# A written-out order table of 1518 operations, replaced by another order of the same operations

## The chip, the cores and the metric

The kernel runs on one core of one Trainium2 chip. The metric is device time in microseconds (us). A core has a matrix engine (TensorE, called PE in the profile, with its weight loads shown apart as PEld), a vector engine (DVE), an activation engine (ACT), a general engine (POOL) and a queue engine for transfers (SP). POOL, SP and ACT can each issue transfers; 16 DMA engines move the data. Each engine runs its own list of instructions in order and waits on semaphores for the others.

## The reference

```python
scores = scale * np.matmul(q, k.transpose(0, 1, 3, 2))      # 8 batches, 8 heads, 576 x 576, head size 64
mask = block_i >= block_j                                   # blocks of 64 positions, causal by block
attn = np.exp(np.where(mask, scores, -1000000000.0) - rowmax)
attn = attn / (np.sum(attn, axis=-1, keepdims=True) + 1e-09)
x = np.matmul(attn, v)                                      # heads side by side: 8 x 576 x 512
h = np.maximum(x.transpose(0, 2, 1) @ w_tok1, 0.0) @ w_tok2 # 576 -> 256 -> 576, over the positions
u = x + h.transpose(0, 2, 1)
h2 = np.maximum(u @ w_ch1, 0.0) @ w_ch2                     # 512 -> 1536 -> 512, over the channels
out = u + h2
```

Attention goes first, then an MLP over the positions (token mixing), then an MLP over the channels. Inputs and output are 32-bit floats; the products run in bf16.

## The kernel before, in words

The kernel goes through the eight batches. For each batch it loads q, k and v, transposes q and k on DVE (L442), forms the scores of each half of the heads in sets on PE (L566), takes their exponentials on ACT (L585 for the first batch, L772 for the others), copies and clears the ends of rows (L594 and L599, on DVE or POOL), multiplies with the values on PE (L616 for a head, L669 for the row ends of a pair of heads) and divides on DVE (L636, L642). Token mixing follows (L807 and L811 up, relu at L793 on ACT or L795 on DVE, then L902 and L933 down), then channel mixing. There, some batches use a plain product (L1030), the others a product with sums of the weights and of the data that needs fewer multiplications (L1103 and L1230 up, L1364 down, with the sums at L1346 and the folds into the output at L1410 on DVE). The output rows leave by the transfers of L1439 and L1455.

Every step is recorded as an operation with a number, the engines that may do it, the operations that it needs, and the PSUM banks that it takes. Nothing runs until the table `ORDER` is read: one word for an operation, with its number, one letter for the engine (T is PE, A is ACT, D is DVE, P is POOL, S is SP), and one letter for each PSUM bank that it takes (a to d the pool "mm", e to h the pool "late", which exists once the scores of the first batch have left s and t). The order of the words is the order in which instructions are emitted, so it is also the order within each engine's list. The reader of the table is this:

```python
for word in ORDER.split():
    digits = word.rstrip("abcdefghstADPST")
    o, letters = self.ops[int(digits)], word[len(digits):]
    o.engine = self.ENGINE[letters[0]]
    ...
    assert all(d.n in done for d in o.deps)
```

So the table alone decides three things: the place of an operation in its engine's list, the engine where there is a choice (a copy out of PSUM may go to ACT or DVE, L400 and L402; a row-end copy to DVE or POOL; an output transfer to SP or ACT), and the PSUM bank.

Operations that are named below: 13, 16 and 19 are the first loads of k and q on SP, with the casts 14, 17 and 20 behind them (L400, L402) and the transposes 15, 18, 21, 23, 25 (L442); 22, 24, 26, 28, 30, 32 and 34 to 43 are further loads on POOL of q, k (L418, L437) and v (L468). 155 to 158 are the loads of the token weights, 159 to 169 and 421 to 437 those of the channel weights and of v and q, k of later batches. 44 is a run of 11 warm-up matmuls (L371), and 45 to 81 are fillers, single matmuls on zeros (L378). 174 is the first score set. 222, 223, 226, 227 are halves of head products of the first batch, 230 the row ends of its pair, and 269 and 281 score sets of the next batch; 281 is the first operation that takes the four late banks. 470 and 445 are score sets of a later batch and 505 a relu. 1037 is the load of the last piece of v of batch 6, 1044 a memset on POOL, 1134 another load. 1568 and 1590 are output transfers, and 1590 is the last operation.

## Time and profile before

| | before |
|---|---|
| median of three runs | 286.15 us (285.68 to 286.21) |
| the profiled execution, its own time | 287.38 us |
| span from the first to the last instruction | 285.6 us |
| PE busy | 275.0 us (96%) |
| weight loads of PE busy | 204.6 us (72%) |
| DVE busy | 238.6 us (84%) |
| ACT busy | 179.2 us (63%) |
| POOL busy | 72.4 us (25%) |
| mean granted clock of PE | 1.000 |

Busy time is the time in which an engine had an instruction in work. The chain of waits is the chain of work that ended last, followed back from the last instruction: at each step to what released it. "issue" in that chain is time in which an engine waited for nothing that the profile shows. A group of instructions has its line, engine, operation, what it writes and reads, the number of them, busy time, mean length of one in ns, and the idle time of the engine ahead of them with its releaser.

### The profile page before, as it was taken

The numbers are of one execution on the slowest core, as the hardware profiler recorded it, in microseconds if no ns is written. First come the engines' busy times: TensorE is split into PE (matmuls) and PEld (weight loads), VectorE is DVE, ScalarE is ACT, GpSimd is POOL, SyncE is SP. The second block draws the span as 40 slices with busy tenths as digits, with TensorE's granted clock in tenths as the row PEclk, the third lists the DMA queues.
The fourth block names the chain that finished last, engine by engine and source line by source line (L and its number), as shares of the span: only waits on it lengthen the run. The fifth ranks groups of instructions, "written<-read, shape, count | busy, mean of one in ns | idle before, by whom it ended". The sixth has DMA issues, their size and how long they took to land.

```text
span 285.6 us, 9588 instructions
## 1 busy us (share of the span) xinstructions
PE 275.0 (96%) x4089; PEld 204.6 (72%) x4110; DVE 238.6 (84%) x515; ACT 179.2 (63%) x331; POOL 72.4 (25%) x126
## 2 busy tenths in 40 slices
PE   8798899999998999999999999999999999999995
PEld 3466557488776777987877657856789976568884
DVE  3587578999898798999998979959897897579984
ACT  3798688962999664897779876073542734652200
POOL 8885661411621171055052120000000000000000
PEclk9999999999999999999999999999999999999999
DMA  7999999964999392999799397011043602100157
GB/s 166 170 171 179 202 191 203 132 107 101 111 93 141 65 141 45 155 222 157 88 102 165 31 181 90 16 61 21 0 76 73 223 0 76 73 2 2 73 149 221
DMA packets 64891, 31.97 MB, mean 112 GB/s; under 512 B 53200, under 2 KB 55888, under 8 KB 64848
## 3 DMA queue, kind: packets, MB, share of 16 engines
q0 software_dynamic: 44896, 17.49, 53.3%
q1 hardware_dynamic: 19520, 13.21, 19.0%
q8 instruction: 32, 0.52, 0.7%
q10 hardware_dynamic: 432, 0.66, 0.7%
q14 instruction: 11, 0.09, 0.1%
HBM read 35.85 MB, written 9.44 MB: 159 GB/s over the span
## 4 chain that ended last, share of the span: by engine, by line
PE 91%; ACT 3%; DMA 2%; issue 2%; DVE 1%; SPq 0%
PE late L1364 23%; PE mm L1103 8%; PE mm L1230 7%; PE mm L566 7%; PE mm L1364 7%; PE late L1230 6%; PE late L1103 6%; PE mm L616 5%; PE mm L807 3%; PE late L616 2%; ACT e_sb L585 2%; PE late L566 2%; PE late L902 2%; PE mm L902 2%; PE late L1030 2%; PE mm L1030 2%
## 5 line engine op out<-in xcount | busy, mean ns | idle before, releaser
L772 ACT ACTIVATE e_sb<-mm 128x512 bf16<-128x512 f32 x82 | 46.6, 607 | 14.0 <-PE late L566 10.2
L772 ACT ACTIVATE e_sb<-late 128x512 bf16<-128x512 f32 x86 | 48.5, 610 | 9.2 <-PE late L566 8.4
L442 DVE STREAM_TRANSPOSE qk_sb<-qk_sb 128x288 int32<-128x288 int32 (+1 forms) x65 | 41.4, 692 | 3.6 <-ACT qk_sb L400 1.6
L468 POOL DMA_DIRECT2D vals<-in_v_dram x45 | 36.9, 830 | 5.7 <-PE mm L616 2.4
L1364 PEld LDWEIGHTS <-gT 128*128 128x128 bf16 x336 | 32.0, 98 | 5.6 <-issue 0.4
L1364 PEld LDWEIGHTS <-sums 128*128 128x128 bf16 x324 | 31.3, 98 | 5.3 <-issue 0.4
L566 PEld LDWEIGHTS <-qk_sb 32*64 32x64 bf16 x1280 | 19.6, 104 | 13.9 <-issue 10.2
L566 PE MATMUL mm<-qk_sb 32*64 32x512 bf16 (+7 forms) x560 | 27.5, 289 | 0.4
L616 PEld LDWEIGHTS <-e_sb 128*128 128x128 bf16 x640 | 23.1, 97 | 6.5 <-issue 3.2
L566 PE MATMUL late<-qk_sb 32*64 32x512 bf16 (+7 forms) x560 | 26.8, 295 | 0.9 <-issue 0.6
L1364 PE MATMUL late<-wd_sb,gT 128*128 128x256 bf16 x168 | 20.7, 273 | 0.0
L1364 PE MATMUL late<-wd_sb,sums 128*128 128x256 bf16 x168 | 20.6, 273 | 0.0
L1103 PEld LDWEIGHTS <-ws_sb 128*128 128x128 bf16 x192 | 18.2, 98 | 3.1 <-issue 0.9
L642 DVE TENSOR_TENSOR x_sb<-mm,rinv 128x256 bf16<-128x256 f32 x45 | 18.7, 421 | 1.3
L616 PE MATMUL mm<-vals,e_sb 128*128 128x65 bf16 x450 | 19.5, 193 | 0.0
L1410 DVE TENSOR_TENSOR o_sb<-late,u_sb 128x512 f32<-128x512 f32 x22 | 14.9, 682 | 3.6 <-PE late L1364 3.6
L1230 PEld LDWEIGHTS <-ws_sb 128*128 128x128 bf16 x120 | 11.7, 98 | 8.6 <-issue 0.2
L1103 PEld LDWEIGHTS <-wc_sb 128*128 128x128 bf16 x144 | 15.3, 114 | 1.4 <-issue 0.4
L1364 PE MATMUL late<-wc_sb,gT 128*128 128x256 bf16 x132 | 16.2, 273 | 0.1
L594 POOL COPY vals<-e_sb 128x256 bf16<-128x256 bf16 (+1 forms) x11 | 4.3, 390 | 41.2 <-ACT e_sb L772 40.5
L400 ACT COPY mm<-late 128x512 f32<-128x512 f32 (+1 forms) x16 | 9.1, 571 | 8.1 <-PE late L1230 5.6
L793 ACT ACTIVATE gT<-mm 128x512 bf16<-128x512 f32 x21 | 12.6, 617 | 1.9 <-PE mm L1103 0.9
(198 smaller groups left out, 628.3 us busy)
## 6 DMA issues: line engine op xcount, KB each, us to landing
out_dram<-o_sb SPq DMA_DIRECT2D x19, 256.0 KB, 2.6
qk_sb<-in_k_dram POOLq DMA_DIRECT2D x14, 288.0 KB, 5.6
qk_sb<-in_q_dram POOLq DMA_DIRECT2D x14, 288.0 KB, 6.0
vals<-in_v_dram POOLq DMA_DIRECT2D x28, 128.0 KB, 4.4
out_dram<-o_sb SPq DMA_DIRECT2D x7, 512.0 KB, 3.5
wc_sb<-in_moe_w_ch_dram POOLq DMA_DIRECT2D x8, 192.0 KB, 7.8
wc_sb<-in_moe_w_ch_dram POOLq DMA_DIRECT2D x3, 512.0 KB, 10.8
vals<-in_v_dram POOLq DMA_DIRECT2D x15, 64.0 KB, 5.2
```

The costliest lines, as they stand in the source:

```text
L442: nc.vector.transpose(dst[:, 0:S, :] .rearrange("p s e -> p (s e)") .bitcast(I32) .rearrange("p (a k) -> p k a", k=NB)[:, k0:k1], raw2.bit ...
L468: nc.gpsimd.dma_start(out=t[128 - p : 128, J, hs, 0:64], in_=src)
L566: nc.tensor.matmul(out=home(n)[64 * half : 64 * half + 64, c : c + w], lhsT=bar[r, 0] if j is None else kT[i][r, 64 * j : 64 * j + 64, par ...
L616: nc.tensor.matmul(out=u[:, I, 0:65], lhsT=e[:, h, c : c + 128], rhs=vt[:, J, head, 0:65], start=(J == 0), stop=(J == I),)
L642: nc.vector.tensor_tensor(out=xt[:, 0:4, 64 * head : 64 * head + 64], in0=u[:, :, 0:64], in1=ri[:, 0:4].to_broadcast([128, 4, 64]), op=MULT,)
L772: nc.scalar.activation(dst, bank_of(x), EXP, scale=scale)
L793: nc.scalar.activation(dst, src, RELU)
L902: nc.tensor.matmul(out=bank_of(bank), lhsT=w2_sb[:, t, 128 * si : 128 * si + 128], rhs=at[:, t, :], start=(t == 0), stop=(t == NDT - 1),)
L1103: nc.tensor.matmul(out=bank_of(bank)[:, 256 * o_ : 256 * o_ + 256], lhsT=x(o_, m), rhs=y[:, :, m, :], start=opens, stop=m == 1, skip_group ...
L1230: nc.tensor.matmul(out=bank_of(bank)[:, 128 * c : 128 * (c + step)], lhsT=x(m), rhs=y[:, c : c + step, m, :], start=opens, stop=m == 1, sk ...
L1364: nc.tensor.matmul(out=bank_of(bank)[:, 256 * i : 256 * i + 256], lhsT=x[:, kk, 128 * i : 128 * i + 128], rhs=y[:, kk], start=first and i ...
L1410: nc.vector.tensor_tensor(out=dst, in0=src, in1=other, op=ADD)
```

## The change

The table is replaced by another one; no function changes. The new table has the same 1518 operations and so the same matmuls, loads and stores. What differs is their order, the choice of the engine for some of them, and the banks. It is three lines shorter, so that lines behind it have numbers lower by three. The diff, cut to the start of the table (some 30 us of work), the places named above, and its end:

```diff
@@ -98,84 +98,81 @@
 ORDER = """
-    13S 5P 9D 2D 3P 16S 44Ta 12P 19S 10P 4P 30P 22P 14D 24P 15D 17A 32P 1D 26P 18D 20A 28P 0A 45Tb 21D 252P 46Tb
-    47Tb 48Tb 49Ta 50Ta 37P 51Ta 52Ta 23D 53Ta 54Ta 25D 55Ta 56Ta 35P 57Ta 7D 174Tst 175T 34P 195A 58Ta 59Ta 60Ta
-    61Ta 196A 62Ta 38P 197D 63Ta 31D 64Ta 65Ta 66Ta 176A 199Tt 36P 177A 178D 67Ta 179D 68Ta 33D 69Ta 255P 70Ta 200A
-    180Ts 27D 198P 71Ta 72Ta 40P 73Ta 181A 29D 182Tt 157P 74Ta 75Ta 76Ta 183A 77Ta 201Ts 43P 78Ta 79Ta 80Ta 253D
-    202A 42P 214Tt 254D 188Tb 189T 41P 215A 184Tc 11D 233Ts 6D 190D 191D 258P 192Td 211Ta 234A 220Tt 216P 256D 39P
-    185T 257D 221A 81Tb 218Ts 155P 212D 213D 207Tb 235D 208T 186D 219A 158P 187D 237Tt 193D 209D 156P 203Ta 210D
-    204T 238A 194D 239Ts 261P 205D 206D 164P 8D 240A 236D 269Tcbda 424P 271A 163P 281Tefgh 270A 166P 259D 273A 217D
-    226Tb 283A 227T 284A 222Tc 223T 228D 241Ta 242T 282A 229D 165P 249Tf 224D 245Tg 285A 225D 162P 246T 230Tb 243D
-    244D 339Tc 159P 250D 231D 232D 337Ta 251D 247D 161P 340A 260D 272A 276Tbfeh 338D 348Tc 262D 160P 278A 349T 263D
...
-    362A 443D 359D 502Te 444P 483A 435P 393D 485A 604P 484A 504Td 503A 437P 170D 486A 470Tcbag 595P 505A 171D 601P
-    473A 445Tfehd 471A 172D 514Ta 448A 508Tc 472A 173D 515A 512Th 506Tb 446A 509D 510Ta 474A 513D 397Tcf 447A 475P
...
-    744A 981D 1022D 966Ta 984A 963Tc 1023D 745T 985A 967D 888D 1119P 986A 964D 965D 983A 1037P 995Td 968D 873A 998Tc
...
-    1056D 1075P 1057D 1015Tc 1134P 1068D 1146A 1127D 1013Ta 1145A 1069D 1102Th 1129D 1147A 1076D 1144A 1014D 1093Td
...
-    1556T 1588A 1567D 1562T 1569S 1557D 1586T 1563D 1568S 1587D 1590S
+    3P 10P 2D 9D 44Ta 45Tb 52Tc 56Td 1D 58Ta 46Tb 13S 14A 16S 15D 17D 18D 54Tc 4P 51Td 19S 12P 62Ta 5P 57Tb 50Tc 22P 23D
+    55Td 20A 21D 59Ta 64Tb 24P 30P 47Tc 25D 48Td 28P 66Ta 174Tst 175T 76Tb 60Tc 176A 177A 70Td 29D 49Ta 43P 74Tb 68Tc
+    71Td 195A 196A 180Ts 197D 75Ta 34P 53Tb 81Tc 26P 181A 198D 32P 182Tt 183A 80Td 37P 65Ta 31D 38P 199Ts 200A 27D 73Tb
+    33D 61Tc 201Tt 178D 35P 179D 202A 36P 188Td 184Ta 189T 190D 214Ts 192Tb 6D 191D 215A 252P 254D 233Tt 234A 185T 186D
+    187D 41P 203Tc 204T 253D 156P 205D 220Ts 221A 40P 211Td 206D 212D 218Tt 158P 219A 67Ta 207Ta 208T 209D 155P 237Ts
+    238A 63Tc 239Tt 255P 240A 78Tc 39P 79Tc 216D 42P 217D 222Tc 223T 213D 69Td 11D 256D 210D 257D 226Ta 193D 194D 157P
+    227T 228D 230Td 229D 281Tefgh 284A 283A 235D 236D 285A 337Tb 224D 225D 339Ta 282A 241Tg 231D 232D 242T 338D 340D
+    269Tcdfb 272A 243D 244D 341Th 261P 262D 263D 342D 245Ta 246T 247D 248D 348Te 349T 351Tg 271A 273A 350A 270A 352T
+    268P 258P 259D 276Tfdhb 164P 353A 280A 278A 249Ta 260D 160P 345Te 279A 346T 250D 251D 343Tc 277A 8D 301Tgabd 305A
...
+    503A 173D 504Tb 505A 470Tcgha 472A 77Te 471A 445Tfdeb 514Tg 512Tc 513D 447A 449A 506Td 508Tb 473A 474A 510Th 515A
...
+    640D 629Ta 630D 631D 572D 632Tb 72Td 573T 574A 635Tg 788Tdfha 791A 689S 633D 634D 790A 673Tc 636D 637D 674D 675D
...
+    993D 751T 994D 1043D 1119P 1036P 1083A 1005D 1006D 742D 752D 1085A 1084A 1045Tcgda 1124D 1046A 1044P 1047A 1049A
+    753T 1134P 1077Tehfc 1081A 1015Tg 1080A 1121D 754D 1078A 755T 1048A 1123D 1016D 1120D 1037P 1058Ta 1079A 1059D 1060D
...
+    1583D 1588A 1584T 1585D 1589A 1563D 1566T 1567D 1569S 1556T 1557D 1568A 1586T 1587D 1590A
 """
```

In numbers: 12 copies out of PSUM, net, go from ACT to DVE, 8 of the clips from DVE to ACT against 2 back, 5 row-end copies or memsets from DVE to POOL against 7 back. Output transfers on ACT's queue are 2 instead of 1 at L1439 and 4 instead of 2 at L1455; the last of all, 1590 (128 KB), is one of them. PE's instructions are the same 4110 pairs of a weight load and a matmul; the number of times that two neighbours on PE use different tile forms (such as 32x64 and 128x128) goes from 120 to 124. POOL issues the early loads in the order 22, 24, 30, 28, 43, 34 (before 30, 22, 24, 32, 26, 28) and so on, with 155, 156 and 158 earlier.

## The prediction

> **What bounds the kernel now.** I read the engine totals and the forty slices first, then the chain of waits, then windows of the stages where the chain leaves PE, and last single lines by form.

> ```profile
> span 285.6 us, 9588 instructions
> PE 275.0 (96%) x4089; PEld 204.6 (72%) x4110; DVE 238.6 (84%) x515; ACT 179.2 (63%) x331; POOL 72.4 (25%) x126
> PE   8798899999998999999999999999999999999995
> PEclk9999999999999999999999999999999999999999
> DMA  7999999964999392999799397011043602100157
> q8 instruction: 32, 0.52, 0.7%
> PE 91%; ACT 3%; DMA 2%; issue 2%; DVE 1%; SPq 0%
> ```

> PE carries 91% of the chain at a full granted clock in every slice. The change keeps PE's 4110 loads of weights and 4110 matmuls, with the same shapes. So only what PE waits for can move: its first operation on real data, gaps on the way, and what follows its last matmul. The chain shows these places (columns: start, length, what):

> ```profile
> 7.34 1.27 DVE qk_sb L442 x3
> 16.61 4.99 ACT e_sb L585 x5
> 21.64 0.66 PE late L566 x15
> 22.29 0.60 issue
> 28.27 1.09 issue
> 51.44 1.08 ACT e_sb L772 x2
> 53.50 0.50 ACT aT L793
> 57.26 1.31 PE late L1364 x12
> 59.15 1.42 PE mm L1364 x12
> 92.01 0.98 issue
> 282.08 0.42 DVE o_sb L1410
> ```

> Three steps are called "issue": PE waits for nothing that the profile shows, in the middle of an operation. Two rows of PE's timeline show where it resumes, and the windows from one stall to the next count its instructions (columns: window, length; then busy time and count of PE, PEld, DVE, ACT, POOL; clock, DMA share, GB/s).

> ```profile
> 22.89 0.38 PE L566 MATMUL late<-qk_sb 32*64 32x512 bf16 x1 [0.60 <-issue]
> 29.36 0.38 PE L855 MATMUL mm<-w_sb,aT 128*128 128x512 bf16 x1 [1.09 <-issue]
> 22.60:28.90 6.30, 5.32 (x127) 4.17 (x128) 4.97 (x17) 4.86 (x10) 3.19 (x6) 1.00 1.09 190
> 28.90:92.60 63.70, 61.93 (x1144) 44.39 (x1151) 55.10 (x128) 51.43 (x102) 24.67 (x40) 1.00 1.13 142
> 220.00:260.00 40.00, 40.00 (x287) 28.64 (x285) 31.56 (x50) 21.86 (x38) 0.00 (x0) 1.00 0.18 67
> 280.00:290.00 10.00, 2.05 (x19) 1.58 (x17) 1.71 (x5) 0.00 (x0) 0.00 (x0) 0.89 0.39 136
> ```

> Between the first two stalls lie 127 + 128 = 255 instructions, between the second and third 1144 + 1151 = 2295, within 9 of 9 x 256. The page's instruction queue moved 32 packets, and PE and PEld together ran 4089 + 4110 = 8199, or 256 for each packet. So I read the stalls as PE arriving at the end of a block of 256 instructions before the next block is there. All three lie where the DMA share of the window is at least 1.09; elsewhere the blocks come in time. From the first stall's end to the second's PE needed 29.36 - 22.89 = 6.47 us for one block.

> **The change part by part.** The sum goes from the profiled execution, 287.38 us with a span of 285.6; the median of the runs, 286.15, is 1.23 below it, and I carry the difference to that median.

> *(a) First score.* The first scores wait for three DVE transposes behind q's cast, 1.27 us in the chain. The new order puts the 160-column one before that cast, so two remain.

> ```profile
> L442 DVE STREAM_TRANSPOSE qk_sb<-qk_sb 128x160 int32<-128x160 int32 x1 | 0.5, 456 | 0.0
> 6.63 0.67 ACT L400 CAST qk_sb<-gT 128x576 bf16<-128x576 f32 x1 [1.47 <-DMA gT<-in_q_dram]
> ```

> That is -0.46 if q's load lands at the same time, and up to +0.5 if POOL's other order of loads (a q piece goes ahead of the pieces of k) slows it; the row shows ACT waiting 1.47 us for it. I take -0.3, nearer the transposes, which are certain.

> *(b) Work ready while ACT does the exps of the first batch.* The exps (4.99 us of chain) set when PE goes on at 21.64. By then the old order has done one more score set; the new one has done four head products and their ends instead, and leaves that set for later.

> ```profile
> 42.97 0.60 PE mm L616 x20
> 24.22 0.32 PE L669 MATMUL late<-vals,e_sb 128*64 128x65 bf16 x8
> ```

> The head products are such a group of 20, 0.60; the ends add about 0.3; a score set costs 0.5 (this one is narrow) to the 0.66 of the row at 21.64. So PE has 0.9 behind it instead of 0.5: -0.4, and as fewer fillers stand between, I take -0.5; bounds -0.9 (the set fits into a later gap) and 0 (the exps end later).

> *(c) The stalls at 22.29 and 28.27.* Blocks stay 256 long, so moving operations changes how much PE time a block holds. A stall is the time from asking for a block to having it, less PE's time until it gets there. I take the asking to be a block and a quarter (320 instructions) ahead, an assumption; then the old stalls answer to latencies of

> ```profile
> 16.27:22.60 6.33, 5.66 (x171) 3.36 (x164) 4.75 (x18) 6.27 (x9) 5.01 (x9) 1.00 1.43 159
> 20.96:28.90 7.94, 6.32 (x179) 4.53 (x160) 5.80 (x19) 6.50 (x13) 4.09 (x8) 1.00 1.12 180
> 85.29:92.60 7.31, 6.43 (x173) 4.59 (x159) 6.44 (x20) 6.75 (x14) 1.61 (x3) 1.00 1.42 145
> ```

> some 6.6, 8.4 and 7.7 us, each window counted on to the resuming matmul (22.89, 29.36, 92.99; the windows' counts take in a few instructions that overlap their start). Adding PE's times per operation along the new order, the 320 instructions ahead of the same two boundaries hold 6.73 and 5.65 us, where the old ones hold 5.04 and 5.59. At the first the new time exceeds the old latency, so no stall; at the second the stall is between 6.6 - 5.65 = 0.95 and 8.4 - 5.65 = 2.75, and I take 1.9, the middle, as which loads stand ahead differs. 1.9 against 0.60 + 1.09: +0.2, bounds -1.69 (no stall at all) and +1.06.

> [...]

> *(d) Other waits from 24 to 31 us.* With work pulled ahead, token-mixing operations meet their DVE copies sooner. In the old window between the stalls PE idles 6.30 - 5.32 = 0.98, of which the stalls' ends are 0.29 and 0.63. Bounds 0 and 0.7, one copy by DVE of 695 ns (row under (k)) that comes late; I take +0.2, as the old order shows nearly none.

> *(e) The wait through ACT at 53.5.* The chain passes over ACT from 51.44 to 54.00, because a relu stands between exps there. In the new order that relu has gone ahead and a filler stands between the two score sets. Bounds 0 and -0.50 (the row); I take -0.3.

> *(f) The stall at 92.01.* The 320 instructions ahead of that boundary hold 6.11 us in the new order, 6.42 in the old, so at the old latency it would be 1.6. But four loads of 288 KB stand queued ahead of it in the old order, from

> ```profile
> 81.24 0.56 POOL L418 DMA_DIRECT2D qk_sb<-in_k_dram  x1 [3.73 <-DVE gT L1157]
> 85.62 0.53 POOL L418 DMA_DIRECT2D qk_sb<-in_q_dram  x1
> ```

> and fewer in the new. Between the bounds of 0 and 2.3 (6.11 against the longest latency) I take 0.4, near the shortest, 6.6: -0.6.

> *(g) Four more changes of PE's tile form* (124 for 120). One costs 1.42 - 1.31 by the two L1364 rows, about 0.1; two fall where PE is full: +0.2.
> *(h) Fillers.* Their number stays, but two now stand at about 48 and 73 us, where PE is full, instead of in the wait for the exps:

> ```profile
> L378 PE MATMUL mm<-wd_sb 128*128 128x256 bf16 x37 | 5.2, 274 | 0.0
> ```

> 5.2 / 37 with overlap leaves some 0.1 each in a row of them: +0.2 (0 if PE would have waited there, as in (e)).
> *(i) A late piece of v.* POOL issues one piece of batch 6's values behind a memset that PE's progress releases, with 6.3 us of PE work until its first use, where 14.6 were. The first of these rows has the median time to landing of such a piece, the second that of a slow transfer on the same queue, and the last two belong to (j):

> ```profile
> vals<-in_v_dram POOLq DMA_DIRECT2D x15, 64.0 KB, 5.2
> wc_sb<-in_moe_w_ch_dram POOLq DMA_DIRECT2D x8, 192.0 KB, 7.8
> out_dram<-o_sb ACTq DMA_DIRECT2D x1, 128.0 KB, 2.5
> out_dram<-o_sb SPq DMA_DIRECT2D x1, 128.0 KB, 2.0
> ```

> By 5.2 it is in time, by 7.8 late by 1.5. +0.2, bounds 0 and 1.5.
> *(j) The last output.* It is issued from ACT's queue instead of SP's: 2.5 against 2.0 us to landing by the last two rows, but ACT is idle from 280 on. +0.1, bounds -0.1 and +0.5. [...]
> *(k) Copies and clips.* A net 12 plain copies from PSUM go from ACT to DVE, some clips and tails the other way:

> ```profile
> L402 DVE COPY mm<-late 128x512 f32<-128x512 f32 x5 | 3.5, 695 | 1.7 <-PE late L1230 1.0 <-PE late L1364 0.7
> L400 ACT COPY mm<-late 128x512 f32<-128x512 f32 x15 | 8.8, 585 | 7.8 <-PE late L1230 5.6 <-PE late L1364 2.2
> ```

> Over the kernel DVE gets about 6 us more (12 by 0.695, less what leaves), nearly all in 220 to 260: 31.56 + 5.8 = 37.4 of 40. PE covers this, being busy for all 40 us there; uncovered, it costs what case 4 says. 0.

> Sum: -0.3 - 0.5 + 0.2 + 0.2 - 0.3 - 0.6 + 0.2 + 0.2 + 0.2 + 0.1 = -0.6; 286.15 - 0.6 = 285.5.

> **The rivals.** *Case 2, no block stalls left.* The new table may also have moved loads away from the asking, so both remaining stalls vanish: -2.67 for the three stalls, and -0.2 for all other terms together: 283.3. For it: most blocks pass without a stall although the DMA engines are full. Against it: 5.65 us before the second boundary is short of every latency in the three windows.
> *Case 3, the blocks come later.* At the upper bounds of (c) and (f), 2.75 and 2.3, these are +1.06 and +1.32, with -0.2 for the rest: 288.3. [...] It decides from a latency of 8 us at the second boundary.
> *Case 4, DVE becomes the bound in 220 to 260.* It has 8.44 us idle there, 2.6 with the added copies. Its waits are for PE's products, which come in order, so part of that idle must stay: with all of it 37.4 + 8.4 - 40 = 5.8 us come on top, with half 1.6, with two thirds 3.0, which I take: 285.5 + 3.0 = 288.5. It decides where the idle cannot fall under 2.6. Against it: PE has no gap in the old window, so the copies have slack.
> *Case 5, nothing on balance.* What leaves one stall arrives in another: 286.15.

> **How the numbers follow.** About 0.2%, 0.57 us, is what a measurement of this kernel can tell from no change. Forecast .45 (own range 284.6 to 286.4, (c) and (f) off by 0.45 each; it splits .28 faster, .13 same, .04 slower); case 2 .18, faster; case 3 .16 and case 4 .12, slower; case 5 .09, same. Faster .46, same .22, slower .32. The range goes from case 2, with (d) and (i) at 0, 282.9, to case 3, 288.3; what lies outside is the far half of cases 3 and 4 and a little of 2.

> **What would show it.** In the new profile: the first scores at about 8.3 (7.34 + 1.27 - 0.3); PE's wait behind the exps ending near 21.3; no "issue" step near 22, one of about 1.9 us near 28, and one under 1 us near 92; no step over ACT near 53; DVE at 37 of 40 busy in 220 to 260 with PE still at 40. The prediction is wrong if the stalls sit at other boundaries or are longer, if PE shows gaps behind DVE late in the kernel, or if PE waits for a value load near batch 6's heads.

## The result, and the profile after

The changed kernel takes 298.31 us (median of 4, 294.95 to 299.17) against 285.91 us for the old one on the same chip: 1.042 times as long, 95% interval 1.033 to 1.050. The forecast was 285.5 us, in a range of 282.9 to 288.3. It is wrong in sign and far outside the range. Executions of one and the same kernel differ in the mean clock that PE was granted and, with it, in time (0.969 to 0.988 in the four of the new kernel), so the clock is given beside a time where that matters.

The profiled execution of the new kernel took 299.17 us. First its page:

```profile
span 297.4 us, 9596 instructions
PE 283.2 (95%) x4088; PEld 208.7 (70%) x4110; DVE 246.2 (83%) x524; ACT 178.9 (60%) x324; POOL 72.9 (25%) x124
PE   8799999999999899999999899999999999999974
PEclk9955999999999999999999999999999999999998
```

PE still does the same matmuls, but it is busy 8.2 us longer, and two of the forty slices of the clock stand at 5 where the old kernel had 9 everywhere. (The chain of this profile can be followed back to 54.7 us only, so its shares are not compared.) The windows of the two places where the clock is low (columns as before: window, length, busy time and count of PE, PEld, DVE, ACT, POOL, then clock, DMA share, GB/s), and of the stretch that case 4 of the prediction was about; the second fence is the old kernel's first place:

```profile
12.00:16.00 4.00, 2.53 (x58) 1.52 (x47) 1.13 (x6) 2.31 (x3) 3.42 (x6) 0.93 1.30 130
16.00:28.00 12.00, 12.00 (x179) 7.51 (x176) 6.80 (x26) 6.55 (x7) 7.69 (x13) 0.50 1.27 188
28.00:32.00 4.00, 3.95 (x104) 3.63 (x103) 2.88 (x9) 3.17 (x7) 2.85 (x5) 0.86 1.42 195
220.00:260.00 40.00, 39.93 (x291) 29.14 (x289) 35.65 (x57) 16.93 (x28) 0.00 (x0) 1.00 0.22 67
284.00:288.00 4.00, 1.96 (x19) 1.52 (x17) 1.58 (x4) 0.00 (x0) 0.00 (x0) 1.00 0.03 9
288.00:292.00 4.00, 4.00 (x24) 2.88 (x23) 2.45 (x7) 0.00 (x0) 0.00 (x0) 0.57 0.47 104
```
```profile
12.00:16.00 4.00, 4.00 (x81) 2.19 (x77) 2.63 (x7) 3.89 (x5) 3.20 (x6) 1.00 1.71 179
16.00:28.00 12.00, 10.98 (x304) 7.79 (x302) 9.06 (x36) 10.66 (x17) 7.97 (x16) 1.00 1.26 173
```

Twice the same picture: a stretch of 4 us in which PE is busy for 2.53 and 1.96 us, and right behind it PE at full business with half a clock. By the trace's record of the clock this lasts 13.65 us the first time (15.44 to 29.09) and 3.41 the second (from 288.50). What PE waited for stands in its timeline, and for the second place in DVE's timeline and in the chain:

```profile
14.98 0.31 PE L613 MATMUL mm<-vals,e_sb 128*128 128x65 bf16 x5 [1.47 <-DMA vals<-in_v_dram]
287.69 2.00 PE L1361 MATMUL late<-wc_sb,sums 128*128 128x256 bf16 x12 [2.04 <-DVE sums L1343]
```
```profile
286.42 0.76 DVE L1407 TENSOR_TENSOR o_sb<-late,e_sb 128x256 f32<-128x256 f32 x2 [3.30 <-DMA out_dram<-o_sb]
```
```profile
96.07 1.35 issue
103.45 0.72 issue
...
158.19 7.44 DMA qk_sb<-in_q_dram
...
281.23 5.00 DMA out_dram<-o_sb
286.42 0.76 DVE o_sb L1407 x2
287.17 0.47 DVE sums L1343
```

So four things are new or larger: a wait for a piece of v at 13.5 us, "issue" stalls near 96 and 103 (the first at the end of the same block of instructions as the old kernel's 0.98 at 92.01, the second new), a late load of q at 158 to 166, and near the end an output transfer of 5 us for which DVE waits, with PE behind it.

To place the loss I set the time at which each of PE's operations starts against the PE work that stands ahead of it in the order (each kind of operation at its own usual length). The difference grows only where PE waits or runs slowly. By this estimate, from 10 to 30 us it grows by 7.4 us in the new kernel and 3.2 in the old one; from 90 to 110 by 2.5 and 1.4; from 160 to 170 by 1.2 and 0; from 270 to the end by 4.3 and 0.

### The profile page after: what moved, and what is told of

It is laid out like the page before. It is cut to its first block, busy times and chain, and to the rows that moved or that the text cites. A ratio compares the mean times of both kernels' runs of the same rounds, so it can differ in the third digit from the quotient of the medians.

```text
span 297.4 us, 9596 instructions
## 1 busy us (share of the span) xinstructions
PE 283.2 (95%) x4088; PEld 208.7 (70%) x4110; DVE 246.2 (83%) x524; ACT 178.9 (60%) x324; POOL 72.9 (25%) x124
## 3 DMA queue, kind: packets, MB, share of 16 engines
q10 hardware_dynamic: 864, 1.31, 1.5%
## 4 chain that ended last, share of the span: by engine, by line
PE 63%; DVE 9%; DMA 4%; issue 3%; POOL 1%; SPq 0%; DVEq 0%
PE late L1361 12%; PE mm L1361 8%; PE late L1227 7%; PE late L1100 6%; PE mm L1100 6%; PE mm L1227 5%; DVE o_sb L1407 3%; PE late L563 3%; DMA qk_sb<-in_q_dram 3%; PE late L613 2%; PE mm L563 2%; PE mm L804 2%; PE mm L613 2%; DMA out_dram<-o_sb 2%; PE mm L899 2%
## 5 line engine op out<-in xcount | busy, mean ns | idle before, releaser
L769 ACT ACTIVATE e_sb<-late 128x512 bf16<-128x512 f32 x92 | 52.7, 611 | 16.8 <-PE late L563 9.2
L769 ACT ACTIVATE e_sb<-mm 128x512 bf16<-128x512 f32 x76 | 43.7, 608 | 8.4 <-PE mm L563 3.9
L439 DVE STREAM_TRANSPOSE qk_sb<-qk_sb 128x288 int32<-128x288 int32 (+2 forms) x65 | 42.3, 693 | 5.7 <-ACT qk_sb L397 3.1
L465 POOL DMA_DIRECT2D vals<-in_v_dram x45 | 37.4, 839 | 18.6 <-PE mm L613 15.2
L563 PE MATMUL mm<-qk_sb 32*64 32x64 bf16 (+7 forms) x522 | 27.4, 287 | 0.6 <-DVE x_sb L639 0.6
L397 ACT COPY mm<-late 128x512 f32<-128x512 f32 x20 | 11.7, 583 | 14.0 <-PE late L1227 6.2
L591 POOL COPY vals<-e_sb 128x256 bf16<-128x256 bf16 x10 | 4.7, 473 | 51.5 <-ACT e_sb L769 40.9
L639 DVE TENSOR_TENSOR x_sb<-mm,rinv 128x256 bf16<-128x256 f32 x36 | 15.0, 419 | 1.0
L582 ACT ACTIVATE e_sb<-sc 128x1024 bf16<-128x1024 f32 (+2 forms) x14 | 11.9, 914 | 6.6 <-PE sc L563 6.6
L1227 PE MATMUL late<-e_sb,ws_sb 128*128 128x512 bf16 (+1 forms) x62 | 14.1, 338 | 0.0
L1407 DVE TENSOR_TENSOR o_sb<-late,u_sb 128x512 f32<-128x512 f32 x16 | 10.9, 684 | 3.5 <-PE late L1361 3.3
## 6 DMA issues: line engine op xcount, KB each, us to landing
vals<-in_v_dram POOLq DMA_DIRECT2D x28, 128.0 KB, 4.9
wc_sb<-in_moe_w_ch_dram POOLq DMA_DIRECT2D x8, 192.0 KB, 7.4
```

The costliest lines, as they stand in the source:

```text
L439: nc.vector.transpose(dst[:, 0:S, :] .rearrange("p s e -> p (s e)") .bitcast(I32) .rearrange("p (a k) -> p k a", k=NB)[:, k0:k1], raw2.bit ...
L465: nc.gpsimd.dma_start(out=t[128 - p : 128, J, hs, 0:64], in_=src)
L563: nc.tensor.matmul(out=home(n)[64 * half : 64 * half + 64, c : c + w], lhsT=bar[r, 0] if j is None else kT[i][r, 64 * j : 64 * j + 64, par ...
L582: nc.scalar.activation(dst, sc[SC.index(note["pool"])][:, :, cols], EXP, scale=scale)
L639: nc.vector.tensor_tensor(out=xt[:, 0:4, 64 * head : 64 * head + 64], in0=u[:, :, 0:64], in1=ri[:, 0:4].to_broadcast([128, 4, 64]), op=MULT,)
L769: nc.scalar.activation(dst, bank_of(x), EXP, scale=scale)
```

## The experiments

All changes below are edits of the order table, if nothing else is said.

**Old start, old end, both.** Three tables spliced from the two: the operations of the first part in one order, and what is left in the other.

```diff
 e1:  old order up to 482, new order for the rest
 e2:  new order up to 1532, old order for the rest
 e4:  old up to 482, new up to 1532, old for the rest
```

> The table runs the old order up to score set 482 (about the first 55 us) and the new order for all that is left. In the profile of the new kernel PE's granted clock is 0.50 from about 15.5 to 28.5 us, after a wait of 1.47 us for a piece of v at 13.5. Theory (the time is lost at three places, of which the start is one): at 30 us the new kernel has lost 3.4 us more than the old one (work done against time passed), so with the old start the clock stays at 1.00 there and the time is 3 to 5 us below that of the new kernel, about 294. Rival (the start only moves a wait that comes later anyway): within 1 us of the new kernel, 298. Rival (all the loss is in the start): about 286.

> The new order up to product 1532 (some 20 us before the end) and the old order for the rest. In the new kernel DVE waits 3.30 us from 283 for an output transfer that still reads the buffer it is to write, PE stands 2.04 us behind it, and its clock then falls to 0.52 for some 3.4 us. Theory: the output rows of the mixed batch leave too late in the new order; with the old end that wait and the slow clock go, 3.5 to 4.5 us less than the new kernel, about 294. Rival (DMA transfers at the end are slow in whatever order): less than 1 us gained.

> Old order up to 482, new order up to 1532, old order for the rest: only the middle (55 to 265 us) is new. Theory (three places): the gains of old start and old end add, some 8 us below the new kernel, about 290; what is left over the old kernel, 3 to 4 us, lies in the middle: stalls without a named cause at 96 and 103 us (1.5 and 0.9, where the old kernel had one of 1.1), and waits near 55 and 168 us (0.5 to 0.9 each). Rival (start and end are all): 286.

Measured: e1 296.55 us, e2 295.23, e4 293.73, against 298.31 for the new kernel and 285.20 for the old one beside them. All three medians are lower, but the sizes are not as expected: e1 gains 1.8 us where 3 to 5 were expected, less than the new kernel's own executions differ, and e4 was to be 290. Its profile, with the clock at 1.00 throughout, has a stall of 2.11 us near 92 us where the new kernel's had 1.35. The chain of e1 has:

```profile
92.52 2.70 issue
...
278.96 5.01 DMA out_dram<-o_sb
```

and the clock of e1 falls behind that stall, from 96 on:

```profile
92.00:96.00 4.00, 1.30 (x26) 1.06 (x23) 2.27 (x8) 1.51 (x4) 0.00 (x0) 0.98 2.82 110
96.00:100.00 4.00, 4.00 (x65) 2.92 (x64) 1.33 (x6) 2.04 (x4) 0.25 (x1) 0.59 0.66 251
```

The 5 us transfer at the end is there again, so it belongs to the new order's end and not to its start. In e2 it is gone. The four executions of e2, which has the new start, are 291.16 us at a clock of 1.000, 293.75 at 0.994, 296.71 at 0.977 and 298.04 at 0.976: the same instructions, slower the lower the clock. The first two alone have a median of 292.46, against the 294 that was expected.

**Fill the wait, leave it as long.**

```diff
-    188Td 184Ta 189T
+    188Td 184Ta 82Tb 83Tc 84Tb ... 94Tb 189T
```

> The new order with 13 more fillers (0.11 us each, 1.4 us) on PE directly ahead of head product 189, the one that waits 1.47 us for v. The piece of v lands no earlier, so the wait itself is as long as before; PE only has work in it. Theory (the cost is the clock, not the wait): the clock stays at 1.00 from 15 to 29 us, and the loss up to 30 us is 3 to 5 us less, about 294. Rival (the clock falls for another reason, such as the many narrow matmuls of this stage): the clock still goes to 0.50, no gain. The 26 added instructions move all later ends of 256-instruction blocks by 26, which may shift the stalls at 96 and 103 us by 1 us or so either way.

Measured 293.32 us (293.00 to 294.68), 5.0 below the new kernel, with clocks of 0.994 to 0.999. The windows of its profile:

```profile
12.00:16.00 4.00, 3.52 (x60) 2.46 (x56) 0.96 (x4) 2.42 (x3) 3.04 (x6) 1.00 1.41 147
16.00:28.00 12.00, 11.33 (x300) 8.47 (x292) 10.10 (x37) 9.72 (x14) 8.21 (x14) 1.00 1.25 177
```

PE does 300 matmuls between 16 and 28 us where the new kernel did 179. Thirteen useless matmuls made the kernel 5 us faster. Not all of that is the start. Compared at the same instruction, PE is 3.7 us ahead of the new kernel's profile at 35 us, the fillers included, and 5.6 at 280, because the stalls near 96 and 103 are shorter too; at the end the clock falls in the new kernel's profile and not in this one. At the start the wait itself costs little; what follows it is the loss.

**The reverse on the old kernel.** Ten fillers are moved from between the first score sets to ahead of them.

```diff
-    ... 71Ta 72Ta ... 73Ta ... 74Ta 75Ta 76Ta ... 77Ta ... 78Ta 79Ta 80Ta
+    ... 57Ta 7D 71Ta 72Ta 73Ta 74Ta 75Ta 76Ta 77Ta 78Ta 79Ta 80Ta 174Tst
```

> The old order, with fillers 71 to 80 moved from between the first score sets (11 to 15 us) into the wait ahead of the first score set. The number of PE's instructions stays, and PE waits for ACT or DMA anyway in both places. Theory (PE idle for about half of some 3 to 4 us near 13 us is enough for the clock to fall, as in the new kernel): the clock goes to 0.50 from 15 us on in most runs, and the time rises by 3 to 6 us, to 288 to 291. Rival (the clock fell in the new kernel for something else): clock 1.00, time within 0.6 us of the old kernel.

Measured: ten executions, four at a clock of 0.976 with 288.2 to 289.1 us, six at 0.994 to 1.000 with 284.8 to 286.4 us (old kernel 285.46). The window of its profile, one of the four:

```profile
16.00:28.00 12.00, 11.72 (x218) 7.68 (x212) 6.27 (x24) 8.57 (x12) 8.39 (x16) 0.50 1.33 193
```

So the clock falls in an old order too, behind gaps of 0.27 and 0.34 us between score sets, in some executions and not in others, for about 3.2 us (medians 288.6 and 285.4). "In most" was too much. Where it does not fall, the fillers' absence costs nothing. The new kernel's five executions have mean clocks of 0.969 to 0.992; that its longer wait makes the fall more likely is argued, not shown.

In the trace's record of the clock the drop comes in portions: 3.41 us near the end of the new kernel's first profile, 13.65 or four times that at its start, and the same kernel differs from run to run. A wait of 1.47 us in a stretch in which PE was busy for 2.53 of 4 us was enough, and in e17 (below) one of 0.62 us with smaller gaps beside it. And in the new kernel PE was busy for all 12 us of the window from 16 to 28, in matmuls of 65 columns or on 32x64 tiles for the greater part, while the clock stayed at 0.50.

What separates falls from holds in these traces is not PE's busy time but how much it streams. Cut each of the nineteen profiles into windows of 3.41 us, the length of the short fall, from the first record of the clock to PE's last matmul, and add up the columns of the matmuls that start in a window, each times the share of a 128x128 tile, the largest form in these traces, that its own tile covers: a filler counts 256, a matmul of a head product 65, the widest of a score set 64. Of 1544 windows, 21 were followed by half a clock. All 21 have sums of at most 3072, and only two of the other 1523 do. PE was busy for the whole window in ten of the 21. On this reading the fall lasts because at half a clock the narrow matmuls of the new kernel's first stage reach only 2374 to 2689 in a window, and thirteen fillers end it because they alone add 3328. That the chip counts this very sum is not shown.

**A buffer of its own.** The fold that waits writes rows of the last batch into the output buffer from which the mixed batch's rows are still being sent. Here the first half of those rows gets other memory.

```diff
     o_sb = ring(3, [128, 2, DM], FP32, "o_sb")
+    o_sb.append(x_sb[2]...bitcast(FP32)...)
...
-            oi.append(out_n[0] % len(o_sb))
+            oi.append(3 if b == B and row == 0 else out_n[0] % 3)
```

> The new order, with the first half of the mixed batch's output rows in a buffer of its own (the third x tile, free by then) instead of one of the ring of three. Nothing else is moved. In the new kernel DVE waits 3.30 us at 283 for the transfer that reads that buffer. Theory (the wait is the write to a buffer that is still being sent): it goes, with PE's 2.04 us behind it and most of the slow clock after it; 3 to 4 us less than the new kernel (298.3), but the start's clock varies from run to run by more than that, so the profile from 270 us on is what counts: PE's end less its start of the last 20 us. Rival (PE waits for the sums, whatever the buffer): the 2.04 us stay.

Measured 295.46 us, 2.85 below the new kernel, although its clock still falls at the start (0.973 to 0.982). At the place where DVE stood for 3.30 us, and on PE where the clock was 0.57:

```profile
281.21 0.76 DVE L1408 TENSOR_TENSOR o_sb<-late,e_sb 128x256 f32<-128x256 f32 x2
```
```profile
284.00:288.00 4.00, 3.72 (x35) 3.09 (x32) 2.67 (x8) 0.00 (x0) 0.00 (x0) 1.00 0.76 187
```

No wait, and a full clock. Compared at the same instruction, PE's lead over the new kernel's profile grows from 1.9 to 4.1 us at the wait and to 5.7 in the 4 us behind it: 2.2 us are the wait and 1.7 the clock. In the old order the last of these rows were sent 3.6 us ahead of the first of the two folds that need their buffer (1579 and 1559) and had landed in 3.5, so that DVE did not wait for them; in the new one they are sent 1.9 us ahead of the folds' turn and take 5.0. The first of the two in the old kernel:

```profile
277.73 0.42 DVE L1410 TENSOR_TENSOR o_sb<-mm,e_sb 128x256 f32<-128x256 f32 x1 [0.16 <-DVE o_sb L1410]
```

**Three loads past a memset.**

```diff
-    ... 1044P 1047A 1049A 753T 1134P ... 1037P ... 1128P ... 1125P
+    ... 1037P 1128P 1125P 1044P 1047A 1049A 753T 1134P
```

> The new order, with three loads (1037: the last piece of v of batch 6; 1128 and 1125: q and k of batch 7) moved on POOL ahead of the memset 1044, which waits 5.42 us for DVE before 156 us. Theory (POOL's order holds the loads back): they are issued some 6 us earlier, the chain's load of q (7.44 us, landing at 165.6) and the 0.6 us wait of PE at 167 go, and PE loses 0.9 us less between 150 and 170. Rival (the loads only take each other's place in full queues): the loss between 150 and 170 stays at 1.2 us or so.

In the new kernel POOL stood at the memset, with the loads behind it; in e6 they go ahead (first fence the new kernel's POOL, second that of e6):

```profile
156.05 0.31 POOL L596 MEMSET e_sb<- 64x256 bf16 x1 [5.42 <-DVE rinv L688]
156.56 1.64 POOL L465 DMA_DIRECT2D vals<-in_v_dram  x2 [0.20 <-issue]
158.19 0.56 POOL L415 DMA_DIRECT2D qk_sb<-in_q_dram  x1
```
```profile
148.99 0.60 POOL L415 DMA_DIRECT2D qk_sb<-in_q_dram  x1
149.54 0.67 POOL L415 DMA_DIRECT2D qk_sb<-in_k_dram  x1
153.78 0.31 POOL L596 MEMSET e_sb<- 64x256 bf16 x1 [3.56 <-DVE rinv L688]
```

PE loses 0.1 us between 150 and 170 us instead of 1.3. The median, 296.58 us, gains 1.7, less than the new kernel's own executions differ, so it is the profile that shows the gain; in it the clock also held at the start, and fell at 94.17 us, in a stall of 3.19 us that began at 91.53.

**All three together, and the stall near 92.**

> The new order with all three edits: 13 fillers in the wait for v ahead of 189, the buffer of its own, and the three loads ahead of the memset. Theory: the filled kernel's 293.3, less about 2 for the end and 1 for the loads, 290.3; what stays above the old kernel (285.2) are 1.4 us of fillers in PE's way as far as v lands earlier, the stalls at ends of blocks near 92 to 104, and waits near 55. Rival (losses hide one another): above 292.

Measured 289.72 us (287.55 to 290.99), close to the 290.3 that was expected, with a spread of 3.4 us at clocks of 0.997 to 0.999. The next edit moves three loads behind another one:

```diff
-    ... 929P ... 926P ... 773P ... 938P
+    ... 938P 929P 926P 773P          (and 928D, 931D back to beside 930D)
```

> The kernel with three edits (289.7), and the loads 929 and 926 (q and k of batch 5, 288 KB each) and 773 (a piece of v) issued on POOL behind the load 938, some 10 us later, with the two transposes of 926 and 929 that stand earliest on DVE moved back beside the others. In the new order these loads are issued right ahead of the end of a block of PE's instructions near 92 us, where the stall was 1.35 to 3.2 us in the profiles with PE's 4110 pairs in place, 0 in the profile of the three edits (its blocks end 26 instructions earlier), whose four times still spread from 287.6 to 291.0. Theory (the fetch of the block waits behind loads issued before it, more in some executions than in others): with the loads behind it the slow executions go, median 287 to 288.5 and a spread under 2 us. Rival (the spread has another cause): median and spread as before, 289.7 and over 3 us.

Measured 288.70 us (288.29 to 288.97). The median falls by 1.0 and the spread from 3.4 to 0.7 us: none of the four is near 291. (Four are not many: e15 below, which differs from e9 in a queue alone, has one of 292.56 us, at a clock of 0.984.) In e9's profile PE is busy through the stretch, at a lower DMA share (the three edits first, e9 second):

```profile
88.00:98.00 10.00, 9.71 (x227) 7.59 (x224) 9.67 (x28) 7.69 (x16) 3.74 (x5) 1.00 1.46 209
```
```profile
88.00:98.00 10.00, 9.95 (x235) 7.99 (x234) 9.60 (x29) 8.15 (x17) 3.67 (x6) 1.00 0.74 166
```

PE gains 0.5 us here. It loses about 0.9 near 116 us that e8 did not lose, and a wait of 0.86 us for v near 172 us, which e8's profile has, is not in e9's. No profile of an execution near 291 was kept, and e8's has no stall at the end of a block, so what the slow ones lost was not seen. The better evidence on the loads is e16 below: with no fillers its block ends at the new kernel's place, and with these loads moved it has no stall there, where all seven profiles with the middle of the new order unchanged and no fillers (the new kernel's two, e1, e2, e4, e5, e6) have 1.1 to 3.2 us. It is one profile, and the old kernel's third (below) has no stall there either, without any such change, so this too is short of a proof. That the stalls are ends of blocks is shown by their places. Between the new kernel's stalls at 96 and 103 us stand 127 + 128 = 255 instructions:

```profile
97.41:103.45 6.04, 5.98 (x127) 4.41 (x128) 4.60 (x11) 3.31 (x7) 3.02 (x4) 1.00 1.33 247
```

and PE's stalls that wait for nothing else, from 0.4 us up and behind the first 7 us, all 24 in the profiles of this study, stand at one place in a block of 256, the 192nd when weight loads and matmuls alone are counted along the program; with the 26 instructions of the fillers they moved by 26 in the order of the work.

**A fourth load.**

```diff
-    ... 1075P 1076P 1135P 1141P 1132P 1133P 1142P 1131P
+    ... 1132P 1133P 1131P 1075P 1076P 1135P 1141P 1142P
```

> As e9, and the loads 1132, 1133 and 1131 (pieces of v of batch 7) moved on POOL to directly behind 1134, ahead of copies and memsets of row ends on which POOL waits. In the profile of the three edits PE waits 0.86 us at 172 for such a piece (6.53 us of the chain). Theory: that wait goes, 0.8 to 1.0 us below e9. Rival (another wait takes its place): within 0.4 us of e9.

Measured 289.26 us against 288.70: nothing gained. The wait near 172 us is absent, but e9's profile does not have it either, so the edit had little left to win. The chain has a new stall at an end of a block, where more loads are now under way (DMA share 1.53 from 155 to 160 us, 0.09 in e9):

```profile
159.54 0.72 issue
```

**The new start alone.**

> The new order up to score set 482, with the 13 fillers in the wait for v, and the old order for all that is left. At 30 us the profile of the three edits stands at 2.99 us lost and 1.42 us of added fillers, the old kernel at 5.90. Theory (the new start is better than the old one once the clock holds; everything later is not): 1 to 1.5 us below the old kernel, 284.0 to 284.5. Rival (the stalls at ends of blocks, shifted by 26 instructions, take it back): 285 to 287.

Measured 286.70 us (285.16 to 289.08, 12 executions) against 285.53: 1.0055 times the old one, interval 1.0027 to 1.0083. The rival holds. The profiled execution, 286.33 us, was below the old kernel's 287.38 as the theory had it, and that comparison misled: the old kernel's first profile was no usual execution.

**The two kernels again.** Both unchanged, to see what a single profile is worth.

> The old kernel unchanged, profiled once more. Its first profiled execution took 287.38 us, 1.9 above the median of its other executions, and held three stalls at ends of blocks (0.60, 1.09 and 0.98 us). Theory (whether a block comes late is a matter of each execution, and most executions of the old kernel have fewer): at least one of the three stalls is missing or under half. Rival (the stalls belong to the order): all three again within 0.3 us each.

> The old kernel unchanged, a third profile, with the same expectations as the second. The stalls, where they are, stand again at the same three ends of blocks.

> The new kernel unchanged, profiled once more. Theory: the wait of PE for v near 13.5 us again lies between 0.4 and 1.5 us, and the clock falls after it only where the wait is long (0.9 or more in the profiles so far); the stall at the end of the block near 92 us is there again (1 us or more), and so is the 2 us wait near the end. Rival (the first profile was an exception): two of the three missing.

The old kernel took 285.70 and 285.93 us. Of the three stalls of its first profile (0.60, 1.09, 0.98), the second profile has the last and the third profile the middle one (first fence the second profile, second fence the third):

```profile
90.42 0.85 issue
```
```profile
27.95 0.65 issue
```

The new kernel took 295.00 us. Its wait at 13.5 us was not there, but a longer one was at 19.5, at head product 222, again for a piece of v; the stall near 92 and the 2 us near the end came back (first fence PE's row, second two windows, third the chain):

```profile
21.98 0.61 PE L613 MATMUL mm<-vals,e_sb 128*128 128x65 bf16 x10 [2.49 <-DMA vals<-in_v_dram]
```
```profile
20.00:24.00 4.00, 2.02 (x39) 1.70 (x46) 2.37 (x8) 0.36 (x1) 1.83 (x4) 0.77 1.26 188
24.00:28.00 4.00, 4.00 (x113) 3.16 (x98) 3.12 (x13) 2.67 (x6) 2.35 (x5) 0.81 1.17 208
```
```profile
92.99 1.12 issue
162.54 0.95 issue
...
277.08 4.98 DMA out_dram<-o_sb
```

Here the clock was low for 3.41 us only (from 22.13), and behind the wait near the end it held. The execution is 4.2 us shorter than the first one and still 9 longer than the old kernel: the long fall of the clock is a part of the loss that comes and goes, and most of the rest stays without it.

**The last output's queue.**

```diff
-    ... 1568A 1586T 1587D 1590A
+    ... 1568S 1586T 1587D 1590S
```

> As e9, with the output transfers 1568 and 1590 (the last one) issued by SP again, as in the old order. In the profile of e9 the last transfer took 3.00 us from issue to landing, in the old one 2.01, with five transfers of the last 4 us on ACT's queue and one on SP's. Theory (ACT's queue holds several transfers that the last must follow): the last lands 0.5 to 1 us earlier after its issue, time 0.5 to 1 us below e9. Rival (the DMA engines are shared, and the queue does not matter): within 0.3 us.

Measured 289.47 us (288.81 to 292.56) against 288.70: no gain. The last transfer took 3.0 us from issue to landing on either queue. What is left of the end's loss, about 0.8 us, was not traced further; the new order sends more of its output in the last 4 us.

**The pieces of v in the order of need,** without the added fillers.

```diff
-    22P 24P 30P 28P 43P 34P 26P 32P 37P 38P 35P 36P 252P 41P 156P 40P 158P 155P 255P 39P 42P 157P
+    22P 24P 30P 28P 34P 26P 32P 36P 35P 37P 38P 43P 252P 41P 40P 39P 42P 255P 156P 158P 155P 157P
```

The line is POOL's own order; other words stand between.

> As e9 (288.7), but without the 13 fillers; instead POOL issues the pieces of v of the first batch in the order in which PE needs them: 36, 35, 37, 38 for the first four heads and then 43, 41, 40, 39, 42 for the others, ahead of the token weights 156, 158, 155 and of the load 255. In the new order 36 landed at 14.94 us (PE waiting from 13.5) and in its second profile 39 landed at 21.94 us (PE waiting 2.49 us from 19.5). Theory (these two pieces are what the new start waits for): both waits fall under 0.5 us, the clock holds without fillers, and the time is 286.5 to 288. Rival (the pieces only change places with k, q and the token weights, which come late instead): as large a wait elsewhere before 30 us, and the clock falls in some executions, 289 or more.

> The start of e16 up to score set 482, then the old order. Against e11 (286.7) it has no added fillers and no wait for v. Theory: 285 to 286, level with the old kernel or 0.5 us below. Rival: 286.5 or more, the start is no better than the old one in whatever order its loads come.

e16 took 288.26 us (288.04 to 288.48), a little above its range, with clocks of 0.998 to 1.000 and no wait for v in the profile:

```profile
12.00:16.00 4.00, 4.00 (x110) 2.77 (x109) 2.17 (x8) 3.99 (x6) 3.39 (x7) 1.00 1.50 139
16.00:28.00 12.00, 11.44 (x284) 7.89 (x282) 10.27 (x36) 10.31 (x16) 7.76 (x14) 1.00 1.17 185
```

So with the loads in the order of need the new start kept its clock, in all four executions. e17 took 285.88 us against 285.02, 1.0033 times (1.0004 to 1.0062): not better than the old kernel. Its start is that of e16, and in one of its twelve executions the clock fell all the same: the profiled one, 289.07 us at 0.976, in which a wait of 0.62 us for v with smaller gaps beside it sufficed (PE's row, then the window):

```profile
13.71 0.19 PE L613 MATMUL mm<-vals,e_sb 128*128 128x65 bf16 x1 [0.62 <-DMA vals<-in_v_dram]
```
```profile
16.00:28.00 12.00, 12.00 (x164) 7.88 (x161) 6.37 (x25) 7.12 (x9) 8.09 (x14) 0.50 1.17 183
```

No version beat the old kernel. Step by step from the new one: 298.31, with the wait filled 293.32, with the end and the three loads mended too 289.72, with the loads near 92 moved 288.70, with v in order instead of fillers 288.26. What is left, 3.2 us above the old kernel, is many small waits in the middle (PE's loss from 30 to 60 us is 1.4 us in e16 against 0.5 in the old kernel's later profiles, 0.9 near 116, 0.9 from 200 on) and the 0.8 at the end. These were not taken apart.

## Why the prediction was wrong

- **The largest loss has no term.** The prediction set out from "only what PE waits for can move" and took PE's clock as full, because it was 9 in every slice of the old kernel. No rival had it fall. Steps (b) and (h) moved just what kept it up: (b) put head products ahead that were "work ready", and they were not, since 189 waits for v piece 36 and, in the second profile, 222 for piece 39. The pieces are not issued later than before (36 at 9.42 us, and at 9.54 in the old kernel's first profile); it is their use that moved ahead of them, 189 from 15.7 to 13.5 us. (h) counted two of the moved fillers, as 0.2 us of cost, when those between the first score sets had held the clock. Measured: 3.7 us by the profiles of e3 and the new kernel (5.0 between their medians, with other gains in it), and 3.2 in the old order (e7). Part (b)'s gain of 0.5 was not seen even where the clock held (e11).
- **The second has none either.** The change moved the mixed batch's output and the folds that reuse its buffer against each other. (j) looked at the last transfer only, for the queue. A write to a buffer that a transfer still reads was not asked for. Measured: 2.85 us between the medians of e5 and the new kernel; by their profiles 2.2 for the wait and 1.7 for the clock behind it, and the second of these did not come in every execution (e13).
- **(f) failed in its choice between the bounds.** The step worked out 1.6 us at the old latency and then took 0.4 "near the shortest", because fewer loads of q and k stand ahead. With two of them, a piece of v and the transposes of L966 ahead of it the stall was 1.35 and 1.12 us in the two profiles, and 1.7 to 3.2 in other kernels with the same middle (e1, e2, e4, e5, e6), to which a fall of the clock can be added (e1, e6). The bound of 2.3 was too low as well.
- **(c) had the mechanism and the wrong stage.** Neither of the two stalls is in the new kernel's two profiles, where the clock was low in this stage. With a full clock, e16 has none either, and e6 had 0.61 us at 27.9 where 1.9 was forecast. The sum also set them against an execution with 2.67 us of stalls; the later profiles of the old kernel have 0.85 and 0.65. Both ends of the terms (c) and (f) moved from one execution to the next. The lead of 320 instructions in them was an assumption that no run shows; in the DMA records of the old kernel's first profile the last packets of 16 KB before the three stalls start at 20.63, 26.93 and 90.68 us and end 1.28, 1.46 and 1.35 us before PE goes on.
- **(a)** was right in direction: first scores at 7.85 and 7.77 us against 8.65 in the first profile of the old kernel, and 7.90 and 8.03 in the later ones. It bought only time to wait for v.
- **(e)** did not come: the wait through ACT gave way to one behind DVE near 55 us, somewhat longer (0.7 us lost from 50 to 60, where the old kernel lost 0.5).
- **(i)** had the right mechanism and was sized 0.2; it measured 1.2 us. Not the piece of v but the load of q queued behind it came out late, which the term did not count.
- **(j)** was close to its estimate: the queue made no difference (e15, 289.47 us against 288.70, with 3.0 us to landing on either queue).
- **(k)** was right: DVE's busy time in 220 to 260 is 35.65 us (37.4 forecast) and PE's 39.93 of 40. Case 4 fell; case 3 was nearest in kind, but its 2.2 us are a sixth of the loss.

## What to carry to other kernels

Where PE's clock has never been seen to fall, ask what keeps it up before moving it: here a wait of 1.47 us in a stage of narrow matmuls cost 3.7 us behind it, and thirteen wide matmuls that do nothing, 1.4 us, were worth more than their time. Before work is pulled ahead, look at when the loads that it needs land. When operations are reordered, check each transfer that an earlier reader must finish with (the last buffers of a ring; 3.30 us of waiting on DVE here) and each load that an in-order queue now puts behind a waiting instruction (POOL's here, 5.42 us at a memset). And profile the kernel before more than once: a stall that is in one execution is not yet a cost of the order.
